# Moving the second attention's first values into the attention, and its row loads to another queue

## The chip, the cores and the metric

The kernel runs on one core of a Trainium2 chip. A core has a matrix engine (TensorE, PE in the profile), three engines for elementwise work (VectorE or DVE, ScalarE or ACT, GpSimd or POOL), and SyncE (SP), which here only issues DMA transfers. Each engine works off its own queue of instructions in order and waits on semaphores for the others. The metric is the device time of one execution in microseconds; the median of several executions is compared.

## The reference

Four blocks run one after the other over x, a matrix of 2048 tokens by 512 features in float32, and each adds its result to x:

```python
x = A_x
x = x + _A_ref(_layernorm(x), A_wqkv, A_wo)
x = x + _B_ref(_layernorm(x), B_wqkv, B_w_phi, B_wo)
x = x + _A_ref(_layernorm(x), A_wqkv, A_wo)
x = x + _B_ref(_layernorm(x), B_wqkv, B_w_phi, B_wo)
```

Block A is softmax attention with 32 heads of 16 features:

```python
qkv = (x @ wqkv).reshape(B, S, 3, H, Dh)           # -> q, k, v by head
scores = einsum("bhqd,bhkd->bhqk", q, k) * Dh ** -0.5
o = einsum("bhqk,bhkd->bhqd", softmax(scores), v)
return o.reshape(B, S, D) @ wo
```

Block B is linear attention. Each head's q and k are mapped by a 16 x 16 matrix w_phi and then by two softmaxes over the 16 features, of the value and of its negative; the state phi_k^T V is 32 x 16 for each head, and the output is phi_q times the state over phi_q times the sum of phi_k, again followed by a product with wo.

## The kernel before

The program has five stages: a preparation with the first layer norm, the first attention (`a1.attention`), the first feature layer (`b1.flow`), the second attention (`a2.attention`) and the last feature layer (`b2.flow`). A generic path behind a condition at the end isn't run on these inputs. Values are kept as a high and a low half in fp16, and a product is three passes (high·high, low·high, high·low), so a product of a 128 x 512 block by four chunks of 128 features is 12 matmuls.

**Attention.** Heads are worked in four octets of eight heads, each as two pairs of half octets ("kq" tiles, group number g from 0 to 7). A step (g, j) takes 512 queries and goes over 16 tiles of 128 keys. For each key tile and each half, `scores` (L1425) writes 128 keys x 2 heads x 512 queries into a pair of PSUM banks, ScalarE takes the exponential into an SBUF tile (L1431, the ring `p` of nine tiles), and `pvs` (L1471) multiplies it with the values. A few of the exponentials are instead computed on VectorE by a polynomial (`power_task`). The kq tiles have 49 rows for each head: 48 rows of high and low halves of the projected keys and queries, which DMAs gather from a staging tile `stg` (`load_rows`, L1402, three DMAs for each of four row groups), and one row with a shift, a bound on the largest score (`load_shift`, L1410). For octet 0 the keys and queries from column AHEAD = 1536 on live in separate small tiles (`kqe`).

The order of all engines inside an attention is written by a planner in the kernel's own Python: it holds estimated costs (`UNIT`, `STEP`, `EXP` and so on), looks 2.6 us ahead and chooses between the next score, the next product with the values, half of one, or a unit of side work. Side work comes from generators (`self.more(...)`): projections of the next octets, the output product of finished tokens, preparation of weights. The strings `LEADS`, `MORES`, `IDLES` and `VBUSY` hold one character for each of the 32 steps (g, j) and each attention: how far ahead a VectorE exponential is placed, the price of an idle TensorE, and how busy VectorE may be.

**Feature layer.** `flow` is a second planner. Each piece of work is a generator that yields an engine ("T" TensorE, "V" VectorE, "A" ScalarE, "P" GpSimd, "D" SP's queue) and a cost; the planner takes the due piece with the lowest rank. The ranks (`RANKS`, `TAIL`, `LAGS`) and strings that put single halves on VectorE or GpSimd (`LOWS`, `ADDS`, `SHARES`, `HALVES`) or choose TensorE, VectorE or GpSimd for a transpose (`TURNS`) are tables. SP isn't one of the engines that this planner orders by itself: its instructions are ordered by the framework below.

The first feature layer ends with the handoff to the second attention. For each block j of 512 tokens: the output product (L2421), the sum into `xt`, layer norm statistics, the normalized rows `xn` (L657 on ScalarE), their transpose into `xnTb` (by TensorE, L670, with ScalarE's high part L680 and VectorE's low part L683; or as an fp16 pair `xh` by a DMA transpose from SP, L2510), the projection of keys and queries of octet 0 (`projected`, L1048, 12 matmuls each), ScalarE's copy `tq` (L2544), VectorE's high and low halves into `stg` (L2547, L2550), ScalarE's squares (L1247). `bounds` sums the squares (L1279), takes the largest (L1285), computes the shift (L1269) and loads it; `rows` loads the kq tiles of the first pair in pieces. `octet_values` projects the values of octet 0 (`values0`, L1233: 48 matmuls of 128 x 128 columns for each j) and copies them out on ScalarE (L1240).

The change touches the planners' tables at the top, `values0`, `values0_out`, the start and the inner choices of `attention`, and `out_block`, `octet_values`, `bounds` and `rows` in `flow`.

## Time and profile before

| what | us |
|---|---|
| median of 3 runs | 2376.18 (2371.74 to 2377.59) |
| the profiled execution, its own time | 2368.89 |
| its span, first to last instruction | 2367.0 |
| TensorE, VectorE, ScalarE, GpSimd busy | 2233.4, 1838.1, 2109.9, 412.0 |

Busy times are sums of records; a matmul's record also covers the time in which it overlaps its neighbours, so a TensorE that is 94% busy isn't 94% used. A row of the order in time gives the start in us from the beginning of the span, the duration, the engine, the source line, the operation, what it writes and reads, and how many equal instructions are merged; in square brackets stand the idle time before it and the work that ended it. A row of groups gives the busy time in us and the mean of one in ns. The profile's chain of waits is empty for this execution, so chains are followed here by hand, from row to row. Line numbers are those of the kernel before; the changed file has its lines three or more further down.

### The profile page before, as it was taken

The page shows a single profiled execution, that of the slowest core. Times are in us where ns is not written, and L with a number is a line of the kernel's source. Part 1 is how long each engine was busy: PE and PEld are TensorE (multiplying, and loading weights), DVE is VectorE, ACT ScalarE, POOL GpSimd, SP SyncE. Part 2 cuts the span into 40 slices and gives each one's busy share as a digit, 9 for nine tenths or more (in the row PEclk, how much of TensorE's full clock was granted, in tenths as well). Part 3 has the DMA queues.
Part 4 walks back from the last instruction along what each step waited for, and adds up shares of the span by engine and source line. Part 5 has one row for each costly group of instructions (what it writes and reads, how often), then busy time and mean ns, then how long its engine had stood idle before and what let it go on. Part 6 is the DMA issues. An engine that isn't in the chain of part 4 may idle for free.

```text
span 2367.0 us, 116770 instructions
## 1 busy us (share of the span) xinstructions
PE 2233.4 (94%) x53046; PEld 1183.4 (50%) x53046; DVE 1838.1 (78%) x2905; ACT 2109.9 (89%) x2415; POOL 412.0 (17%) x536
## 2 busy tenths in 40 slices
PE   6999999999999999999789999999999999999988
PEld 4555555544545554455445554555455545454443
DVE  8567646989687778899855798789977777568997
ACT  6899999999999999766658999999999999996663
POOL 3100000000000000289750000000000000004975
PEclk9999999999999999999999999999999999999999
DMA  5410431123133632143353003302310531223334
GB/s 192 83 23 8 83 53 53 31 45 69 52 66 76 197 94 83 47 107 81 87 129 56 16 17 48 45 4 45 46 45 13 107 115 55 74 67 95 68 59 136
DMA packets 241922, 163.92 MB, mean 69 GB/s; under 512 B 151832, under 2 KB 219016, under 8 KB 240520
## 3 DMA queue, kind: packets, MB, share of 16 engines
q1 hardware_dynamic: 240232, 153.60, 28.8%
q8 instruction: 417, 6.83, 1.2%
q0 software_dynamic: 1184, 2.77, 0.3%
q14 instruction: 89, 0.73, 0.1%
HBM read 62.16 MB, written 41.94 MB: 44 GB/s over the span
## 4 chain that ended last, share of the span: by engine, by line


## 5 line engine op out<-in xcount | busy, mean ns | idle before, releaser
L1425 PE MATMUL s<-kq 49*32 49x512 f16 x14688 | 774.8, 381 | 63.3 <-ACT p__1018 L1431 3.9
L1425 PEld LDWEIGHTS <-kq 49*32 49x32 f16 x15872 | 381.2, 89 | 686.1 <-issue 570.1
L1178 POOL PARTITION_ALL_REDUCE nma<-nmx x6 | 6.3, 1058 | 990.6 <-DVE nmx L1175 815.5
L2062 PEld LDWEIGHTS <-xnTa 128*128 128x128 f16 x1152 | 110.8, 98 | 132.3 <-issue 3.4
L2062 PE MATMUL fl<-wbqk,xnTa 128*128 128x512 f16 x576 | 130.8, 379 | 1.6 <-DVE f L2141 1.6
L1431 ACT ACTIVATE p__1017<-s 128x1024 f32<-128x1024 f32 x119 | 127.8, 1074 | 0.3 <-PE s L1425 0.2
L1431 ACT ACTIVATE p__27883<-s 128x1024 f32<-128x1024 f32 x114 | 122.4, 1074 | 1.9 <-PE s L1425 1.6
L1431 ACT ACTIVATE p__1020<-s 128x1024 f32<-128x1024 f32 x114 | 122.5, 1075 | 0.0
L1431 ACT ACTIVATE p__27887<-s 128x1024 f32<-128x1024 f32 x112 | 120.9, 1079 | 1.7 <-PE s L1425 1.6
L1431 ACT ACTIVATE p__27884<-s 128x1024 f32<-128x1024 f32 x112 | 120.4, 1075 | 1.1 <-PE s L1425 1.0
L1431 ACT ACTIVATE p__27882<-s 128x1024 f32<-128x1024 f32 x112 | 120.5, 1075 | 1.1 <-PE s L1425 1.0
L1431 ACT ACTIVATE p__27881<-s 128x1024 f32<-128x1024 f32 x109 | 117.3, 1076 | 3.7 <-PE s L1425 3.6
L1431 ACT ACTIVATE p__1016<-s 128x1024 f32<-128x1024 f32 x110 | 118.1, 1073 | 1.3 <-PE s L1425 1.0
L1431 ACT ACTIVATE p__1019<-s 128x1024 f32<-128x1024 f32 x110 | 118.1, 1074 | 0.8 <-PE s L1425 0.6
L1431 ACT ACTIVATE p__1018<-s 128x1024 f32<-128x1024 f32 x108 | 116.4, 1078 | 2.0 <-PE s L1425 1.9
L1431 ACT ACTIVATE p__1021<-s 128x1024 f32<-128x1024 f32 x109 | 116.8, 1071 | 0.2
L1431 ACT ACTIVATE p__1022<-s 128x1024 f32<-128x1024 f32 x108 | 115.8, 1073 | 0.4 <-PE s L1425 0.3
L1431 ACT ACTIVATE p__27885<-s 128x1024 f32<-128x1024 f32 x104 | 111.3, 1070 | 2.6 <-PE s L1425 2.5
L1431 ACT ACTIVATE p__27886<-s 128x1024 f32<-128x1024 f32 x104 | 111.7, 1074 | 0.7 <-PE s L1425 0.4
L1431 ACT ACTIVATE p__1015<-s 128x1024 f32<-128x1024 f32 x103 | 110.6, 1074 | 1.8 <-PE s L1425 1.6
L1431 ACT ACTIVATE p__27889<-s 128x1024 f32<-128x1024 f32 x101 | 108.7, 1076 | 0.0
L1509 DVE SCALAR_TENSOR_TENSOR xt<-double,c_oA,xt 128x512 f32<-128x512 f32 x72 | 53.5, 743 | 70.5 <-PE double L771 69.5
(701 smaller groups left out, 7213.0 us busy)
## 6 DMA issues: line engine op xcount, KB each, us to landing
kq<-stg SPq DMA_DIRECT2D x168, 128.0 KB
xd<-xt SPq DMA_DIRECT2D x112, 128.0 KB
xt<-xd SPq DMA_DIRECT2D x80, 128.0 KB
xt<-xd SPq DMA_DIRECT2D x20, 512.0 KB
v<-vyt SPq DMA_DIRECT2D x384, 16.0 KB
oD<-osp SPq DMA_DIRECT2D x48, 128.0 KB
ob<-oD SPq DMA_DIRECT2D x48, 128.0 KB
xd<-xt SPq DMA_DIRECT2D x12, 512.0 KB
```

The costliest lines, as they stand in the source:

```text
L1178: nc.gpsimd.partition_all_reduce(mm, m, P, bass_isa.ReduceOp.max)
L1425: nc.tensor.matmul(banks2[u][32 * c:32 * c + 32, :], self.side(g, half, 64 * u, 0, kt * P + 32 * c, 32), self.side(g, half, 64 * u, 1, j * ...
L1431: nc.scalar.activation(pt, s, AF.Exp, scale=EXPS)
L1509: nc.vector.scalar_tensor_tensor(xt[:, u, :], ps[h], con["oA"], xt[:, u, :], op0=ALU.mult, op1=ALU.add)
L2062: nc.tensor.matmul(ps, xnT[:, a, c, t * P:(t + 1) * P], w(b, c), start=(i == 0 and c == 0), stop=(i == 2 and c == NC4 - 1))
```

## The change

1. The values of octet 0 of the second attention are no longer projected in the first feature layer. `octet_values` is gone, and `attention` of the second layer starts its side work with a new generator `first_values`: four pieces of 12 matmuls for each j, and a copy on VectorE instead of ScalarE. The planner lets a product with the values wait for the block that it needs.
2. The row loads and the shift's constant half for the first pair (`rows`) go out on ScalarE's queue, the third piece on ScalarE's and GpSimd's; they were on SP's and, for that piece, SP's and GpSimd's. `rows` gets the lowest rank (2000 instead of 0).
3. SP's queue takes part in the feature planner: DMA issues yield "D" with a cost, for row loads, shift loads, xt loads and stores.
4. The attention's strings have two characters for each step instead of one (64 instead of 32), and all tables have new values. In the first attention 978 exponentials stay on ScalarE; in the second it is 966 instead of 967.

```diff
-TURN, FOLD = 0.85, 1.15
+TURN, FOLD, VALUE = 0.85, 1.15, 0.85
...
-LOWS = "VVVVPPPPPPVPVVVP", "VVVVVVVPVVVPVPPV"
+LOWS = "VVVVPPPPPPVPVVVP", "PVPVVVPPVVPPPVPV"
...
-HALVES = "VPPPPPPPPPPPVPPP", "PPPPPPPPPPPPPPPP"
-TURNS = "VTPPPTTTPTVTPPVVTTTT", "TPPTVPPTVTVPPPVPPPTP"
+HALVES = "VVPPPPPPPPPPVPPP", "PPPPPVPPPPPPPPPP"
+TURNS = "TTPVTTTTVVVTVTTTTTTT", "VPPPTTTTTVPPPPTTVVPP"
...
+        def first_values(self):
+
+            for j in range(NJ):
+                yield "M", 4
+                idx, ps = self.take()
+                for t in range(4):
+                    yield "pe", VALUE, True
+                    self.values0(j, ps[0], (t,))
+                self.spawn(self.first_out(j, idx, ps))
+
+        def first_out(self, j, idx, ps):
+
+            yield "V", 0.61, 0
+            self.values0_out(j, ps[0], nc.vector.tensor_copy)
+            self.freed(idx)
+            self.done[("v", j)] = self.plan.end + 0.15
...
+            if self.li:
+                self.more(self.first_values())
             for o in (1, 2, 3):
                 self.more(self.octet(o))
...
-                        vnext = [[(G, kt, 0), (G, kt, 1)] for G, kt in islice(pvq, 4)]
+                        vnext = [[(G, kt, 0), (G, kt, 1)] + [("v", kt // 4)] * (self.li and G < 2 * NJ) for G, kt in islice(pvq, 4)]
...
-            def octet_values(j):
-                yield known(state_, "begun")
-                yield known(halves, (j, 0), (j, 1))
-                b = yield "T", 2.75, "one"
-                nxt.values0(j, one(b))
-                yield "A", 0.5
-                nxt.values0_out(j, one(b))
-                F.give_bank(b)
...
-                        nxt.load_shift(0, slice(0, AHEAD), None, (1,), (nc.sync, nc.gpsimd))
+                        yield from shift_of(0, slice(0, AHEAD), None, (1,), "SG")
+                        state_["first"] = F.end + 2.0
...
-                nxt.load_rows(0, slice(AHEAD, S), nxt.kq_end)
-                nxt.load_shift(0, slice(AHEAD, S), nxt.kq_end)
+                yield from rows_of(0, slice(AHEAD, S), nxt.kq_end)
+                yield from shift_of(0, slice(AHEAD, S), nxt.kq_end)
...
+            ISSUE = dict(S=nc.sync, G=nc.gpsimd, A=nc.scalar)
+
+            def rows_of(g, sl, tiles=None, queues="S"):
+                stg = nxt.oct[g // 2]["stg"]
+                for t, r, h8 in nxt.pair_rows(g, tiles, sl):
+                    src = stg[h8 * DH:(h8 + 1) * DH, :, sl]
+                    q = queues[(r // 64) % len(queues)]
+                    if q == "S":
+                        yield "D", 1.95
+                    elif q == "A":
+                        yield "A", 0.6
+                    for n, part in enumerate((slice(1, 3), slice(1, 4, 2), slice(0, 3, 2))):
+                        ISSUE[q].dma_start(t[r + 16 * n:r + 16 * n + 16], src[:, part, :])
...
             def rows():
                 yield known(evac, *[(j, ten) for j in (0, 1) for ten in (1, 0)])
+                yield "D", 2.5
                 nxt.next_w = nxt.octet_w(1)
                 yield F.got(2, "big")
                 F.take("big"), F.take("big")
-                nxt.load_head(False)
+                nxt.alloc_pairs(0)
+                nxt.oct[0]["sh"] = nxt.shift_tile()
+                yield from rows_of(0, slice(0, 1024), None, "A")
+                yield from shift_of(0, slice(0, AHEAD), None, (0,), "A")
                 yield known(evac, (2, 1), (2, 0))
-                nxt.load_rows(0, slice(1024, AHEAD), None, (nc.sync, nc.gpsimd))
+                yield from rows_of(0, slice(1024, AHEAD), None, "AG")
...
-                    F.add(rows(), 0)
+                    F.add(rows(), 2000.0)
...
-                        F.add(octet_values(j), rank("values", j))
```

`shift_of` does for the shift row what `rows_of` does for the rows, at "D" 0.72 or "A" 0.2 for each DMA.

Three places show how instructions move. The first is ScalarE's queue at the handoff, before the change, from the copies of the last block's rows on (xh: fp16 rows for a DMA transpose, tq: projected keys or queries, sq: squares, v: first values):

```order
L2504 ACTIVATE xh<-xn 128x512
L2544 ACTIVATE tq_27618<-fm_24209,c_qk 128x512
L680 ACTIVATE xnTb_2_27579<-fm_24209 128x4x128
L1247 ACTIVATE sq<-stg 128x512
L2544 ACTIVATE tq_27657<-fl,c_qk 128x512
L1247 ACTIVATE sq<-stg 128x512
L2544 ACTIVATE tq_27675<-fm_24209,c_qk 128x512
L1247 ACTIVATE sq<-stg 128x512
L2544 ACTIVATE tq_27729<-fl,c_qk 128x512
L1247 ACTIVATE sq<-stg 128x512
L1240 ACTIVATE v_25865<-fm_24209 128x16x32 x2
L1431 ACTIVATE p__27881<-s 128x1024
```

and now, from the last pair of normalized rows on (L2637 and L2648 are the row and shift loads, L2574 is tq, L2534 is xh, L684 the high part of a TensorE transpose):

```order
L661 ACTIVATE xn<-xt,lb,ly 128x512 x2
L2637 DMA kq_0_27510<-stg 16x2x1024 x3
L2534 ACTIVATE xh<-xn 128x512
L2574 ACTIVATE tq_27548<-fm_24231,c_qk 128x512
L2637 DMA kq_0_27510<-stg 16x2x1024 x3
L684 ACTIVATE xnTb_2_27482<-fm_24230 128x4x128
L1268 ACTIVATE sq<-stg 128x512 x2
L2637 DMA kq_1_27511<-stg 16x2x1024 x6
L2648 DMA kq_0_27510<-sh 1x3x512 x2
L2648 DMA kq_1_27511<-sh 1x3x512 x2
L2574 ACTIVATE tq_27603<-fm_24230,c_qk 128x512
L1268 ACTIVATE sq<-stg 128x512
```

Sixteen DMA issues stand between the last normalized rows and the first of the last two products; another product, its squares and six more row loads follow, and then the first exponential. The copies of the values are gone.

The second place is SP's queue there. Before, from the first pair's row loads on (kq_0_27558 and kq_1_27559 are the first pair, kq_0_27851 the second):

```order
L1402 DMA kq_0_27558<-stg 16x2x1024 x6
L1402 DMA kq_1_27559<-stg 16x2x1024 x6
L1410 DMA kq_0_27558<-sh 1x3x512 x2
L1410 DMA kq_1_27559<-sh 1x3x512 x2
L2510 DMA_TRANSPOSE xnTb_2_27579<-xh 128x8x128 x2
L1402 DMA kqe<-stg 16x2x512 x12
L1410 DMA kqe<-sh 1x16x32 x2
L1402 DMA kq_0_27558<-stg 16x2x512 x3
L1402 DMA kq_1_27559<-stg 16x2x512 x3
L1410 DMA kqe<-sh 1x16x32 x2
L1410 DMA kq_0_27558<-sh 1x3x512
L1410 DMA kq_1_27559<-sh 1x3x512
```

and now (first pair kq_0_27510 and kq_1_27511, second pair kq_0_27681):

```order
L2648 DMA kqe<-sh 1x16x32 x2
L2540 DMA_TRANSPOSE xnTb_2_27482<-xh 128x8x128 x3
L2637 DMA kqe<-stg 16x2x512 x12
L2648 DMA kqe<-sh 1x16x32 x2
L1431 DMA kq_0_27681<-sh 1x4x512 x2
L205 DMA wA<-dA 128x512 x4
L1423 DMA kq_0_27681<-stg 16x4096
L1423 DMA kq_0_27681<-stg 16x2x2048
L2648 DMA kq_0_27510<-sh 1x3x512
L2648 DMA kq_1_27511<-sh 1x3x512
```

The transposes of the last block stand ahead of all row loads; the first pair's last shift rows stand behind the kqe rows, four weight loads and two loads of the second pair.

The third place is VectorE at the start of the second attention, before (sh: the shift; vyt: values of octet 1):

```order
L1294 TENSOR_REDUCE top<-nmt 1x1
L1266 TENSOR_SCALAR okt<-top 1x1
L1268 TENSOR_SCALAR neg<-top 1x1
L1269 TENSOR_SCALAR sh<-sh,neg 1x512
L1120 COPY vyt_28060<-double 128x512
L1122 TENSOR_TENSOR vyt_28060<-vyt_28060,double 128x512
```

and now:

```order
L1290 TENSOR_SCALAR sh<-sh,neg 1x512
L1261 COPY v_25858<-double 128x16x32
L1261 COPY v_25858<-pm_27832 128x16x32
L1261 COPY v_25858<-pm_27942 128x16x32
L1261 COPY v_25858<-pm_28021 128x16x32
L1124 COPY vyt_28443<-pm_28111 128x512
L1126 TENSOR_TENSOR vyt_28443<-vyt_28443,pm_28112 128x512
```

Four copies of the first values stand ahead of octet 1's. On TensorE, whose rows alternate with weight loads, the first values stand behind the first score: nine scores with eight groups of 12 matmuls between them, a product with the values, two scores, 48 matmuls, a product, two scores, 48 matmuls, a product.

61 lines of the change are left out of this document (41 added, 20 removed).

## The prediction

> **What bounds the kernel now.** I read the table of stages first, then the waits of ScalarE, then the order in time of every queue across the handoff from the first feature layer to the second attention. The five stages are cut at the first and last exponential of each attention. The columns are the window, its length, the busy time of TensorE, its weight loads, VectorE, ScalarE and GpSimd, the granted TensorE clock, the DMA share and the rate.
>
> ```profile
> 71.50:980.70 909.20, 875.25 (x24374) 468.83 (x24374) 663.15 (x1049) 901.56 (x978) 12.57 (x29) 1.00 0.29 66
> 980.70:1246.20 265.50, 240.47 (x2185) 123.80 (x2191) 228.81 (x383) 157.28 (x242) 198.70 (x279) 0.97 0.41 92
> 1246.20:2148.80 902.60, 867.47 (x24311) 458.50 (x24299) 690.89 (x1018) 891.98 (x967) 12.86 (x25) 1.00 0.24 51
> 2148.80:2367.00 218.20, 200.67 (x1832) 98.25 (x1820) 196.84 (x307) 118.88 (x169) 162.37 (x143) 0.96 0.39 89
> ```
>
> Both attentions are bound by ScalarE: 978 and 967 exponentials fill 901.56 of 909.20 and 891.98 of 902.60 us, 0.922 us each in the second, which leaves 10.6 us of idle time there. The two feature layers are bound by no single engine. The first is 265.5 us long, and its end is a chain of waits:
>
> ```profile
> 1223.30:1229.50 6.20, 0.00 (x0) 0.00 (x0) 1.12 (x2) 1.30 (x2) 0.00 (x0) 0.75 0.48 92
> 1229.50:1246.20 16.70, 14.33 (x148) 8.98 (x156) 5.72 (x18) 3.83 (x6) 4.82 (x14) 0.89 0.30 54
> ```
>
> For 6.2 us TensorE does nothing, and afterwards it runs at a lower clock. What it waits for stands in SP's queue (start, duration, what was issued):
>
> ```profile
> 1214.02 7.83 SPq L1402 DMA_DIRECT2D kq<-stg  x12
> 1221.95 2.89 SPq L1410 DMA_DIRECT2D kq<-sh  x4
> 1224.95 2.66 SPq L2510 DMA_TRANSPOSE xnTb<-xh  x2
> 1227.72 7.82 SPq L1402 DMA_DIRECT2D kqe<-stg  x12
> ...
> 1243.30 1.40 SPq L1410 DMA_DIRECT2D kq<-sh  x2
> 1244.74 0.56 SPq L1402 DMA_DIRECT2D kq<-stg  x1
> ```
>
> Twelve row loads take 0.65 us each to issue, and the same 0.65 us for half the bytes (kqe), so it is the issue that costs, not the transfer. A shift load takes 0.72, a transpose 1.33. The last two transposes of the last block's normalized rows stand behind 16 loads that nothing needs yet. On TensorE:
>
> ```profile
> 1220.00 0.66 PE L670 MATMUL fm<-ident,xn 128*128 128x128 f32 x4
> 1220.49 2.75 PE L1048 MATMUL fl<-xnTb,wA 128*128 128x512 f16 x12
> 1229.55 4.56 PE L1048 MATMUL fm<-xnTb,wA 128*128 128x512 f16 x12 [6.30 <-DMA xnTb<-xh]
> 1233.95 2.75 PE L1048 MATMUL fl<-xnTb,wA 128*128 128x512 f16 x12
> 1236.54 2.84 PE L1233 MATMUL fm<-wAv,xnTb 128*128 128x128 f16 x48
> 1239.31 0.82 PE L1279 MATMUL fl<-sq,bones 128*32 128x512 bf16 x3
> ...
> 1245.56 0.80 PE L1425 MATMUL s<-kq 49*32 49x512 f16 x16 [2.32 <-DVE sh L1269]
> ```
>
> The keys' projection waits 6.30 us for those transposes and then takes 4.56 us where its twins take 2.75. The values of one block (48 matmuls, 2.77 us from start to start) stand ahead of the norms (L1279) that give the bound, without which no score can start. On ScalarE:
>
> ```profile
> 1217.33 1.52 ACT L657 ACTIVATE xn<-xt,lb,ly 128x512 f32<-128x512 f32 x2 [0.46 <-POOL lb L2464]
> ...
> 1234.15 0.69 ACT L2544 ACTIVATE tq<-fm,c_qk 128x512 f32<-128x512 f32 x1 [9.06 <-PE fm L1048]
> ...
> 1237.92 0.63 ACT L1247 ACTIVATE sq<-stg 128x512 bf16<-128x512 f16 x1 [0.49 <-DVE stg L2547]
> ...
> 1246.20 1.02 ACT L1431 ACTIVATE p__27881<-s 128x1024 f32<-128x1024 f32 x1 [2.65 <-PE s L1425]
> ...
> 1260.71 1.02 ACT L1431 ACTIVATE p__27885<-s 128x1024 f32<-128x1024 f32 x1
> ```
>
> I call the end of the last pair of normalized rows Z, here 1217.33 + 1.52 = 1218.85. From Z to the first exponential are 27.35 us, and this is the stretch that the change rewrites.
>
> **The change, part by part.** *The handoff after Z.* Three chains now race, and the latest decides.
>
> The work itself: a TensorE transpose, ScalarE's high part and VectorE's low part take from 1220.00 to the end of this row, 2.47 us:
>
> ```profile
> 1221.80 0.67 DVE L683 TENSOR_TENSOR xnTb<-fm,xnTb 128x512 f16<-128x512 f32 x1
> ```
>
> Then 12 matmuls, 2.75. So the first of the last two products is ready at Z+5.3 (before: 1234.15, Z+15.3). From there to the first exponential it took 12.05 us, of which the norms lost 0.76 behind the values (last square done 1237.92 + 0.63 = 1238.55, norms 1239.31); without them 11.3. That is Z+16.6, a gain of 10.7 us.
>
> ScalarE's queue: between the last xn and that product it has sixteen issues, six row loads ahead of the high part, then six more and four shift loads. The trace has no DMA issue on ScalarE. The lower bound is nothing on the path (it issues while it would wait), the upper is SP's price for each, 12 × 0.65 + 4 × 0.72 = 10.7, or more if the queues disturb each other. GpSimd's own row loads are nearest beside SP's:
>
> ```profile
> 1238.18 3.22 POOL L1402 DMA_DIRECT2D kq<-stg  x6 [18.39 <-DVE stg L2547]
> ```
>
> that is 0.54 each. I take SP's price, since it is the same kind of queue, and a start when the xn pair starts (Z-1.5): the product is then read at Z+9.2, and the first exponential comes at Z+20.5.
>
> SP's queue: from about Z+1.5 (the last fp16 half) it issues one transpose, twelve kqe rows, four shift loads (kqe and the next pair), six larger loads (four weights, two rows of the next pair), and only then the shift row that the first score needs: 1.33 + 12 × 0.65 + 4 × 0.72 + 6 × 0.56 + 0.72 = 16.1, so Z+17.6. Before, the score came 0.86 after these issues (1243.30 + 1.40 to 1245.56), and the exponential 0.64 after the score: Z+19.1, and up to 1.5 more, since that shift load waits for a load ahead of it to land.
>
> Both queues say Z+19 to Z+21; I take Z+20.2, a gain of 7.1, with ends of 10.7 (queues free) and -6 (queues disturb each other, below).
>
> *Ahead of Z.* TensorE loses one projection and one block of values before the last output product, 2.75 + 2.77, and gets three transposes more, 3 × 0.66: 3.5 us less. VectorE gets one more low half of the queries and two more low parts of transposes, by these rows:
>
> ```profile
> L2263 DVE TENSOR_TENSOR fq<-f,fq 128x1024 f16<-128x1024 f32 x2 | 2.9, 1450 | 0.0
> ...
> L683 DVE TENSOR_TENSOR xnTb<-fm,xnTb 128x512 f16<-128x512 f32 x4 | 2.6, 678 | 0.0
> ```
>
> 1.45 + 2 × 0.68 = 2.8 us more, while two divisions move to GpSimd. VectorE has 228.81 of 265.5 us to do and no cover over long stretches, so Z moves by -3.5 to +2.8; I take -1.
>
> *First values inside the second attention.* Four blocks of 48 matmuls, 11.1 us by the 2.77, move behind the first score. In the new order nine scores alternate with eight quarters of a block; then come a product with the values, two scores, a whole block, and the same again. The rates (a product of all 512 columns is two halves):
>
> ```profile
> 1250.75 0.54 PE L1425 MATMUL s<-kq 49*32 49x512 f16 x8
> 1250.97 0.74 PE L1471 MATMUL pm<-p__27881,v 64*32 64x512 f32 x4
> ...
> 1251.83 0.54 PE L1425 MATMUL s<-kq 49*32 49x512 f16 x8
> ```
>
> Score 0.22, product 0.86, quarter 0.69, block 2.77. The 14th score starts 9 × 0.22 + 8 × 0.69 + 3 × 0.86 + 4 × 0.22 + 2 × 2.77 = 16.5 us after the first, and its exponential 0.64 later: 17.1, against 1260.71 - 1245.56 = 15.15 now. So +2.0. The rest of the 11.1 us takes the place of the next octet's values, which start later and are due far later. The cover is TensorE's slack; if it is gone, ScalarE pays all 11.1. The four copies out of the bank go from ScalarE to VectorE, which is busy 690.89 of 902.6 us. One exponential fewer stands on ScalarE (966): -0.9.
>
> *Tables.* The first attention keeps 978 exponentials and the same order over its first 600 scores: 0, at most 1 either way. In the last layer VectorE gives four low halves of values to GpSimd (4 × 0.68 by the row of their shape) and takes one of queries (1.45): 1.3 less on an engine busy 196.84 of 218.2 us, where GpSimd fills up. I take -0.5, bounds -2.5 and +1.5.
>
> The sum is -1 - 7.1 + 2.0 - 0.9 - 0.5 = -7.5. I round it to -7, for the rest of the tables can only lose what nobody has seen. The profiled execution took 2368.89 (span 2367.0) and would take 2362; the median of the three runs is 7.3 above it, so the forecast for the median is 2376.18 - 7 = 2369.2.
>
> **Rivals.** *The queues are no hindrance:* ScalarE's sequencer issues in its waits, SP overtakes. Then 10.7 after Z and 3.5 ahead of it: -3.5 - 10.7 + 2.0 - 0.9 - 0.5 = -13.6, 2362.6. For it speaks that ScalarE works 157.28 of 265.5 us there; against it, that SP's order is fixed and long.
>
> *The issues on ScalarE and SP hold each other up.* From Z-1.5 on sixteen issues on ScalarE and some twenty on SP stand side by side, and each queue's loads wait on loads of the other. If they go out one at a time, 36 × 0.65 = 23.4 us, ScalarE reads the first product at about Z+22 and the first exponential comes at Z+33: 6 later than now, in all -1 + 6 + 2.0 - 0.9 - 0.5 = +5.6, 2381.8. It decides from about 1.1 us per issue on ScalarE on: sixteen of them then end at Z+16, and the gain is gone. For it speaks SP's timeline, where twelve issues stand end to end from 1214.02 to 1221.85 and nothing overlaps; against it, that the six loads on GpSimd at 1238.18, issued while SP was issuing too, took no longer each than SP's. [...]
>
> *TensorE has no slack in the attention:* it is busy 867.47 of 902.6 us, so ScalarE waits for all 11.1 us: -1 - 7.1 + 11.1 - 0.9 - 0.5 = +1.6, 2377.8. Against it: those records overlap (the score row lasts 0.54, but the next starts after 0.22), and ScalarE idles only 10.6 us now.
>
> *The handoff is gated elsewhere anyway:* the order of the SP queue isn't what the code asks for, and the bound's shift row lands late, say at Z+25. Gain 2.3 there: -2.4 in all, 2373.8.
>
> **How the numbers follow.** What a measurement of this kernel can tell from no change is about 0.3%, 7.1 us. The forecast gets 0.45 (from -11 to -3, half of it beyond -7.1), the free queues 0.20, the gated handoff 0.15, no slack 0.08, queues in each other's way 0.12 (-1 to +12, half of it beyond +7). Faster: 0.20 + 0.23 = 0.43; slower: 0.06, and 0.04 for tables that go wrong in stages that I took at 0: 0.10; the same: 0.47. The range reaches from the free queues to just short of the queues in each other's way, 2361 to 2380; the forecast's own is 2365 to 2373.
>
> **What would show it.** Right: no wait of TensorE for a transpose at the handoff, first exponential 19 to 21 us after Z, ScalarE's issues at 0.6 to 0.7 us, the first values as 192 short matmuls behind the first score, about 5 us of ScalarE's idle time among its first 14 exponentials, and 966 of them in 904 us. Wrong: issues on ScalarE near 0.2 us with the first exponential before Z+18, or above 1.1 us with one after Z+27; a second attention longer than 908 us; a Z that moved by more than 4 us; a last layer that moved by more than 3.

## The result, and where the time went

The changed kernel takes 2394.23 us (median of four, 2391.45 to 2399.25), the kernel before 2376.89 beside it. The ratio is 1.0091 (95% interval 1.0079 to 1.0104): slower by 17 us by the medians and 22 by the ratio, where I had forecast 7 us less. The stages of the changed kernel, cut as before at the first and last exponential of each attention:

```profile
71.74:994.12 922.38, 879.79 (x24405) 471.20 (x24406) 663.67 (x1052) 902.28 (x978) 12.69 (x29) 0.99 0.29 65
994.12:1268.52 274.40, 234.05 (x1995) 114.57 (x1994) 234.88 (x388) 155.87 (x237) 192.13 (x274) 0.93 0.38 88
1268.52:2182.67 914.15, 876.39 (x24760) 472.49 (x24762) 700.00 (x1023) 891.18 (x966) 12.18 (x25) 0.99 0.24 50
2182.67:2397.50 214.83, 199.53 (x1828) 97.81 (x1816) 194.01 (x305) 121.54 (x172) 164.78 (x145) 0.96 0.41 92
```

Against before: the first attention +13.3 us (922.4 for 909.1, with the same 978 exponentials), the first feature layer +8.9 (Z comes 243.9 us after the end of the attention, not 238.2; from Z to the first exponential 30.5, not 27.4), the second attention +11.5 with one exponential fewer, the last layer -3.4. With 0.2 ahead of the first exponential that sums to 30.5 us: this profiled execution is the longest of its kernel (2399.25) and the one of before was a short one (2368.89), so some 10 us of it are chance. Part of this lies in the first attention: the kernel before and seven of the kernels below have the same instructions there, in the same order on ScalarE, VectorE, GpSimd and SP, and take 909.1 to 915.2 us.

*The two attentions.* The waits of ScalarE and VectorE name two places. First ScalarE's, then VectorE's rows, then SP's queue at the first place, in the changed kernel (the line numbers are 4 to 21 higher than before's, 30 in the feature layer):

```profile
818.81 1.02 ACT L1452 ACTIVATE p__1020<-s 128x1024 f32<-128x1024 f32 x1 [7.23 <-PE s L1446]
1949.66 1.03 ACT L1452 ACTIVATE p__27717<-s 128x1024 f32<-128x1024 f32 x1 [7.33 <-PE s L1446]
```

```profile
815.44 1.29 DVE L1462 TENSOR_SCALAR px<-pm 128x512 int32<-128x512 f32 x2 [10.40 <-DMA wbqk<-dBqk]
...
1946.29 1.29 DVE L1462 TENSOR_SCALAR px<-pm 128x512 int32<-128x512 f32 x2 [9.37 <-DMA xd<-xt]
```

```profile
802.74 8.03 SPq L205 DMA_DIRECT2D wbqk<-dBqk  x14
810.86 2.17 SPq L205 DMA_DIRECT2D xd<-xt  x2
```

VectorE starts an exponential of its own in a buffer (px) that comes out of the same ring as the tiles of x (xt). The rows of an earlier xt are still to be stored, and the store stands behind fourteen weight loads that take 8.03 us to issue. VectorE waits 10.40 us, TensorE finds its bank not emptied, and ScalarE loses 7.23 us. The second attention has a wait of the same kind at 1946.29; the store is issued at 1943.44 there, 6.5 us after the rows were summed, behind weight loads and other loads and stores. The longest wait at such a row in the attentions of before is 1.81 us.

*The handoff.* ScalarE's queue and its work, then SP's queue, then TensorE, all of the changed kernel:

```profile
1236.54 0.72 ACTq L2637 DMA_DIRECT2D kq<-stg  x1
1237.26 0.80 ACT L661 ACTIVATE xn<-xt,lb,ly 128x512 f32<-128x512 f32 x1
...
1242.86 1.36 ACTq L2637 DMA_DIRECT2D kq<-stg  x2
...
1246.11 1.31 ACTq L2637 DMA_DIRECT2D kq<-stg  x2
1249.42 0.59 ACTq L2637 DMA_DIRECT2D kq<-stg  x1
1250.44 0.59 ACTq L2637 DMA_DIRECT2D kq<-stg  x1
1252.10 1.25 ACTq L2637 DMA_DIRECT2D kq<-stg  x2
1253.44 3.70 ACTq L2648 DMA_DIRECT2D kq<-sh  x4
1257.24 0.69 ACT L2574 ACTIVATE tq<-fm,c_qk 128x512 f32<-128x512 f32 x1 [11.35 <-DMA wA<-dA]
...
1268.52 1.02 ACT L1452 ACTIVATE p__27711<-s 128x1024 f32<-128x1024 f32 x1 [7.77 <-PE s L1446]
...
1289.78 1.03 ACT L1452 ACTIVATE p__27715<-s 128x1024 f32<-128x1024 f32 x1 [2.30 <-PE s L1446]
```

```profile
1239.17 4.50 SPq L2540 DMA_TRANSPOSE xnTb<-xh  x3
1243.77 7.83 SPq L2637 DMA_DIRECT2D kqe<-stg  x12
```

```profile
1246.33 4.72 PE L1052 MATMUL fm<-xnTb,wA 128*128 128x512 f16 x12 [7.57 <-DMA xnTb<-xh]
...
1267.56 0.86 PE L1446 MATMUL s<-kq 49*32 49x512 f16 x8 [4.38 <-DVE top L1315]
1268.35 1.46 PE L1254 MATMUL double<-wAv,xnTb 128*128 128x128 f16 x12
...
1274.21 0.84 PE L1254 MATMUL double<-wAv,xnTb 128*128 128x128 f16 x12
```

The transposes are all issued by Z+5.6 (before: Z+8.8; Z is 1238.06 here), but TensorE still waits 7.57 us for them, and the first product is ready at 1251.05, Z+13.0, where I had said Z+5.3. It is read only at 1257.24, Z+19.2, since ScalarE's sixteen issues last from 1236.54 to 1257.14. The issues themselves are not slow: each of the twelve row loads takes 0.59 to 0.73 us on ScalarE, and SP's twelve beside them keep their 0.65. The time goes by between them: 3.45 us before 1242.86, 1.89 before 1246.11, then 2.00, 0.43 and 1.07 among the last six. In the trace the loads of SP and ScalarE signal on the same eight semaphores (GpSimd's on eight others), and these issues carry a wait on the semaphore that they then use. By the landings in the trace, the issues at 1249.42, 1250.44 and 1252.10 go out 0.02 us after the kqe load of SP that used their semaphore last has landed, that at 1242.86 as long after one of SP's transposes, and that at 1246.11 as long after ScalarE's own load of 1242.86. From the read product to the first exponential it is 11.28 us; I had said 11.3. The 14th exponential starts 21.26 us after the first, where before had 14.51: a quarter of a block takes 1.46 us at first and 0.84 later, and the granted clock of the changed kernel says why:

```profile
1253.60:1257.10 3.50, 0.04 (x1) 0.06 (x1) 0.00 (x0) 0.00 (x0) 0.00 (x0) 1.00 0.49 124
1257.10:1274.20 17.10, 8.82 (x72) 4.56 (x71) 5.64 (x18) 5.59 (x7) 4.82 (x14) 0.50 0.43 76
...
1276.50:1279.00 2.50, 2.50 (x50) 1.68 (x48) 0.00 (x0) 2.50 (x3) 0.00 (x0) 1.00 1.17 125
```

The clock falls to 0.50 at 1257.1, 3.5 us into TensorE's wait for tq, stays there through the norms and the wait of 4.38 us behind them, and is 0.50 for the first 6.6 us of the scores. In before, too, it is 0.59 over the first 3.8 us of the second attention.

### The profile page after: what moved, and what is told of

The parts are those of the page before. It is cut to its first block, busy times and chain, and to the rows that moved or that the text cites. A ratio compares the mean times of both kernels' runs of the same rounds, so it can differ in the third digit from the quotient of the medians.

```text
span 2397.5 us, 117355 instructions
## 1 busy us (share of the span) xinstructions
PE 2238.4 (93%) x53346; PEld 1188.8 (50%) x53346; DVE 1850.8 (77%) x2915; ACT 2111.0 (88%) x2412; POOL 407.2 (17%) x533
## 4 chain that ended last, share of the span: by engine, by line
ACT 40%; PE 30%; DVE 12%; issue 10%; POOL 5%; SPq 2%; DMA 1%; ACTq 0%; DVEq 0%; POOLq 0%
PE s L1446 7%; PE double L1492 6%; PE pm L1492 5%; ACT p__1016 L1452 3%; ACT p__1020 L1452 2%; ACT p__1017 L1452 2%; PE pm L775 2%; ACT p__1019 L1452 2%; ACT p__1018 L1452 2%; ACT p__27716 L1452 2%; ACT p__1023 L1452 2%; ACT p__1021 L1452 2%; ACT p__1022 L1452 2%; ACT p__27717 L1452 2%; ACT p__27713 L1452 2%
## 5 line engine op out<-in xcount | busy, mean ns | idle before, releaser
L1452 ACT ACTIVATE p__1020<-s 128x1024 f32<-128x1024 f32 x115 | 123.5, 1074 | 8.0 <-PE s L1446 8.0
L1452 ACT ACTIVATE p__27711<-s 128x1024 f32<-128x1024 f32 x113 | 121.2, 1073 | 8.9 <-PE s L1446 8.8
L1452 ACT ACTIVATE p__1017<-s 128x1024 f32<-128x1024 f32 x118 | 126.6, 1073 | 2.1 <-PE s L1446 1.9
L1452 ACT ACTIVATE p__27716<-s 128x1024 f32<-128x1024 f32 x118 | 126.6, 1073 | 1.1 <-PE s L1446 1.1
L1452 ACT ACTIVATE p__1016<-s 128x1024 f32<-128x1024 f32 x116 | 124.5, 1073 | 2.0 <-PE s L1446 1.7
L1452 ACT ACTIVATE p__27713<-s 128x1024 f32<-128x1024 f32 x114 | 122.3, 1073 | 3.5 <-PE s L1446 3.4
L1452 ACT ACTIVATE p__27717<-s 128x1024 f32<-128x1024 f32 x110 | 118.2, 1074 | 7.8 <-PE s L1446 7.7
L1452 ACT ACTIVATE p__1021<-s 128x1024 f32<-128x1024 f32 x111 | 119.0, 1072 | 1.4 <-PE s L1446 1.2
L1452 ACT ACTIVATE p__27719<-s 128x1024 f32<-128x1024 f32 x110 | 118.2, 1075 | 0.7 <-PE s L1446 0.5
L1452 ACT ACTIVATE p__27718<-s 128x1024 f32<-128x1024 f32 x108 | 115.9, 1074 | 0.8 <-PE s L1446 0.7
L1452 ACT ACTIVATE p__1018<-s 128x1024 f32<-128x1024 f32 x106 | 113.9, 1075 | 2.5 <-PE s L1446 2.5
L1452 ACT ACTIVATE p__27715<-s 128x1024 f32<-128x1024 f32 x104 | 111.6, 1073 | 4.4 <-PE s L1446 4.2
L1452 ACT ACTIVATE p__1022<-s 128x1024 f32<-128x1024 f32 x106 | 113.6, 1072 | 2.0 <-PE s L1446 1.9
L1452 ACT ACTIVATE p__1019<-s 128x1024 f32<-128x1024 f32 x106 | 113.6, 1072 | 0.8 <-PE s L1446 0.6
L1452 ACT ACTIVATE p__1015<-s 128x1024 f32<-128x1024 f32 x103 | 111.0, 1077 | 1.8 <-PE s L1446 1.7
L1452 ACT ACTIVATE p__27714<-s 128x1024 f32<-128x1024 f32 x98 | 104.9, 1071 | 2.5 <-PE s L1446 2.2
L1452 ACT ACTIVATE p__1023<-s 128x1024 f32<-128x1024 f32 x97 | 104.0, 1072 | 0.5 <-PE s L1446 0.3
L2087 PE MATMUL fl<-wbqk,xnTa 128*128 128x512 f16 x444 | 101.2, 379 | 0.0
```

What stands on the lines that cost most here:

```text
L1452: nc.scalar.activation(pt, s, AF.Exp, scale=EXPS)
L2087: nc.tensor.matmul(ps, xnT[:, a, c, t * P:(t + 1) * P], w(b, c), start=(i == 0 and c == 0), stop=(i == 2 and c == NC4 - 1))
```

## The experiments

Times are medians; each ratio is to the kernel before, run beside it. The stages are those of one profiled execution each: "Z" is counted from the end of the first attention, "to exp" from Z to the first exponential.

| kernel | us | ratio (95%) | att. 1 | Z | to exp | att. 2 (exps) | last |
|---|---|---|---|---|---|---|---|
| before | 2376.89 | | 909.1 | 238.2 | 27.4 | 902.6 (967) | 218.2 |
| changed | 2394.23 | 1.0091 (1.0079-1.0104) | 922.4 | 243.9 | 30.5 | 914.2 (966) | 214.8 |
| q_sp | 2394.65 | 1.0093 (1.0077-1.0108) | 919.0 | 242.8 | 27.4 | 915.5 (966) | 214.7 |
| q_pool | 2404.76 | 1.0122 (1.0105-1.0138) | 923.9 | 243.5 | 36.3 | 915.9 (966) | 214.9 |
| w_pool | 2385.02 | 1.0047 (1.0033-1.0060) | 914.2 | 243.5 | 30.5 | 909.3 (966) | 215.0 |
| act_rows | 2377.23 | 1.0021 (1.0012-1.0030) | 910.6 | 251.0 | 23.6 | 899.5 (967) | 217.9 |
| fv_only | 2387.92 | 1.0065 (1.0052-1.0079) | 910.5 | 242.7 | 31.2 | 913.2 (974) | 216.9 |
| old_exp | 2387.71 | 1.0065 (1.0051-1.0078) | 910.7 | 242.5 | 31.2 | 910.7 (974) | 215.1 |
| old_flow | 2400.15 | 1.0123 (1.0107-1.0139) | 918.8 | 245.2 | 23.5 | 911.9 (966) | 224.4 |
| late | 2366.13 | 0.9976 (0.9966-0.9987) | 910.4 | 238.3 | 22.9 | 899.8 (967) | 216.9 |
| warm | 2382.28 | 1.0041 (1.0028-1.0055) | 913.4 | 237.7 | 27.5 | 910.5 (974) | 217.2 |
| no_fv | 2403.73 | 1.0131 (1.0115-1.0146) | 918.9 | 253.3 | 20.8 | 917.0 (976) | 219.7 |
| late_f2 | 2366.67 | 0.9980 (0.9971-0.9989) | 911.8 | 238.5 | 21.2 | 903.1 (967) | 217.1 |
| late_f2w | 2367.29 | 0.9976 (0.9964-0.9987) | 911.4 | 238.9 | 21.1 | 904.9 (967) | 216.8 |
| mended | 2396.15 | 1.0108 (1.0094-1.0123) | 911.1 | 251.8 | 19.1 | 922.2 (966) | 217.0 |
| mended_cold | 2393.70 | 1.0095 (1.0080-1.0110) | 911.7 | 242.4 | 24.3 | 918.7 (966) | 217.7 |
| fv_warm | 2396.98 | 1.0107 (1.0092-1.0121) | 915.2 | 244.4 | 34.6 | 911.1 (974) | 216.5 |
| fv_fill | 2390.35 | 1.0078 (1.0065-1.0091) | 911.8 | 239.5 | 35.4 | 910.9 (974) | 218.2 |
| mended2 | 2382.61 | 1.0038 (1.0024-1.0052) | 912.7 | 243.3 | 25.0 | 914.1 (966) | 217.2 |

**The loads of the handoff on another queue, in the changed kernel: q_sp, q_pool.**

```diff
-            ISSUE = dict(S=nc.sync, G=nc.gpsimd, A=nc.scalar)
+            ISSUE = dict(S=nc.sync, G=nc.gpsimd, A=nc.sync)      # q_sp;  A=nc.gpsimd: q_pool
```

> The changed kernel, with the sixteen loads that it issues from ScalarE's queue at the handoff (and the six behind them) put on SP's queue; the order on TensorE, VectorE and ScalarE is the same. In the changed kernel ScalarE is held from 1236.54 to 1257.14 us by these issues (1.21 us each beside SP's, 0.6 to 0.8 alone) and reads the first of the last two products 19.2 us after the last normalized rows (Z). Theory: an issue on ScalarE costs its own time and more beside SP's, and blocks the evacuations. Then this kernel's ScalarE is free, but SP has 16 issues more ahead of the last transposes (10.7 us at 0.65 each), so the end of the handoff moves from Z+30.5 to about Z+27, as in the kernel before: 3 us less than the changed kernel. Rival: what counts is the number of issues, on whatever queue, since they go out one at a time: no difference, Z+30. The two long stalls of VectorE in the attentions stay in both cases.

> The changed kernel, with the same loads on GpSimd's queue. GpSimd issued six such loads in 3.21 us (0.54 each) while SP was issuing too. Theory (ScalarE's queue and SP's hold each other up, GpSimd's does not): ScalarE reads the first product at about Z+8 and the first exponential comes 19 to 21 us after Z, where the changed kernel has 30.5: some 10 us less in all. Rival (issues go out one at a time whatever the queue): SP's twelve loads get slower than 0.65 each and the first exponential stays at Z+28 or later: within 3 us of the changed kernel.

On SP the profile does what the theory says: tq is read 15.3 us after Z and the first exponential comes at Z+27.4. The time is that of the changed kernel all the same (1.0093 for 1.0091), as the rival has it; 3 us are near what these runs can tell apart, so this run decides nothing. On GpSimd both were wrong: it is 7 us slower by the ratios, 10 by the medians. GpSimd issues its loads in 0.54 each, but SP's transposes beside them take 1.33, 3.12 and 4.70 us to issue, where the changed kernel has 1.28 to 1.71, and the keys' projection waits 13.57 us (SP, GpSimd, TensorE of q_pool):

```profile
1240.11 9.30 SPq L2540 DMA_TRANSPOSE xnTb<-xh  x3
```

```profile
1238.78 5.95 POOL L2637 DMA_DIRECT2D kq<-stg  x11
```

```profile
1253.27 5.28 PE L1052 MATMUL fm<-xnTb,wA 128*128 128x512 f16 x12 [13.57 <-DMA xnTb<-xh]
```

**The loads alone on ScalarE, in the kernel before: act_rows.**

```diff
-            self.load_rows(0, slice(0, 1024))
+            self.load_rows(0, slice(0, 1024), None, (nc.sync,) if every else (nc.scalar,))
...
-                nxt.load_rows(0, slice(1024, AHEAD), None, (nc.sync, nc.gpsimd))
+                nxt.load_rows(0, slice(1024, AHEAD), None, (nc.scalar, nc.gpsimd))
```

(and the shift loads behind the first likewise)

> The kernel before, with only its row loads (and the four shift loads behind them) moved from SP's queue to ScalarE's at the same place of its program; compute order as before. Theory: SP's last transposes come up to 10 us earlier, but ScalarE's issues beside SP's cost 0.7 to 1.2 us each and block it for 15 to 20 us, so the first exponential comes 27 to 32 us after Z (before: 27.35): 0 to 5 us slower than the kernel before. Rival (the queue change is a gain by itself, and the loss of the changed kernel comes from its tables alone): first exponential 17 to 22 us after Z, 5 to 10 us faster than before.

5 us slower, as the theory had it, but by another way: the issues block ScalarE ahead of Z, so Z comes 12.8 us later, and the rest is shorter. ScalarE's queue of act_rows, with the normalization that stands behind the issues:

```profile
1215.44 5.38 ACTq L1402 DMA_DIRECT2D kq<-stg  x8
1223.23 2.52 ACTq L1402 DMA_DIRECT2D kq<-stg  x4
1229.30 0.81 ACT L657 ACTIVATE xn<-xt,lb,ly 128x512 f32<-128x512 f32 x1 [13.11 <-DMA kq<-sh]
```

Each issue takes 0.59 to 0.72 us, so the price that I had taken from SP holds on ScalarE. Between the eighth and the ninth it waits 2.41 us; a shift load of SP, issued at 1220.70, landed at 1223.20, 0.03 us ahead of the ninth. Put ahead of Z, even issues at that price hold the normalization up by 13.11 us.

**Weight loads off SP's queue: w_pool; the old exponentials' tables: old_exp** (both from the changed kernel; old_exp has MORES, IDLES and VBUSY of before in the same way, each sign doubled).

```diff
-            spread(self.wqk.rearrange(...), dBqk.rearrange(...), 8, 2)
+            spread(self.wqk.rearrange(...), dBqk.rearrange(...), 8, 2, nc.gpsimd)     # w_pool
...
-LEADS = ("bb775577777777777799777766aa7777aa557777a97777446777550077000000", ...)
+LEADS = ("bb775577777777777799777766aa7777aa557777aa7777447777550077000000", ...)    # old_exp
```

> The changed kernel, with the sixteen loads of the second layer's query and key weights (wbqk) issued from GpSimd's queue instead of SP's, in both attentions; the planned order is the same but for these. Theory: VectorE's waits of 10.40 us at 815.44 and 9.37 us at 1946.29 are waits for a buffer whose rows are still to be stored, and the store stands in SP's queue behind those loads (1 load each 0.6 us); each costs ScalarE 7.2 to 7.3 us. Without the loads ahead of it the store goes out some 8 us earlier, both stalls nearly vanish, and the kernel gets 12 to 15 us faster than the changed one, some 2380. Rival: the stores land late for another reason (the transfers themselves, or the loads ahead of these): the stalls stay, and less than 4 us is won.

> The changed kernel with the exponentials' tables of before (each entry written twice), all else as changed; it has 974 exponentials in the second attention instead of 966. Theory: the stall at 815 us in the first attention comes from the new tables, which start a task of VectorE where its buffer's rows still wait in SP's queue behind sixteen weight loads: with the old tables the first attention takes 909 to 912 us again instead of 919 to 924, and the second loses its stall of 7 us but gets 7 us of exponentials. In all some 10 us faster than the changed kernel. Rival (the stall comes with the first half of the program for another reason, the tables are innocent): the first attention stays above 917 us.

Both show the cause in the first attention, and both win less than expected: w_pool 10 us by the ratios instead of 12 to 15, old_exp 6 instead of 10. In w_pool the store is issued at 801.72 with no weight load ahead, VectorE's wait is gone in the first attention and still 6.06 us in the second, where loads of ob remain in the queue, and ScalarE waits 0.66 and 3.41 us in place of 7.23 and 7.33:

```profile
801.72 2.87 SPq L205 DMA_DIRECT2D xd<-xt  x4
```

```profile
1933.02 1.29 DVE L1462 TENSOR_SCALAR px<-pm 128x512 int32<-128x512 f32 x2 [6.06 <-DMA ob<-oD]
```

With the old tables the first attention is at 910.7. Between the 780th and the 840th exponential the changed kernel loses 8.0 us to before; q_sp, q_pool, no_fv and old_flow, the other four with the new tables and those loads on SP, lose 7.0 to 9.1, and the thirteen without the one or the other at most 0.9.

**The move of the first values alone, in the kernel before: fv_only.**

```diff
+            if self.li:
+                self.more(self.first_values())
...
-                        F.add(octet_values(j), rank("values", j))
```

(with the new functions first_values, first_out and values0 of the change)

> The kernel before, with only the first values moved into the second attention (queues and tables of before; the planner then gives ScalarE 974 exponentials there instead of 967). Theory: their cost is paid at the start of the attention, where TensorE runs at a low clock after the wait of the handoff: the 14th exponential starts 5 to 7 us later after the first than the 14.51 us of before, of which 4 to 5 us stay; the seven exponentials add 6.4 us; the handoff gets 2 to 4 us shorter without the values. In all 5 to 10 us slower than before. Rival (TensorE has the slack, the move is free or a gain): the 14th exponential at most 3 us later, the attention at most 909 us, the kernel within 3 us of before or faster.

The loss is larger than the theory's, 15.5 us: 6.4 for seven exponentials, 4.2 for the rest of the attention as expected, but the feature layer is 8.4 us longer, not shorter, though it has 192 matmuls fewer. My first reading was TensorE's clock (0.63 and 0.83 in stretches of 20 us where before had 0.83 and 1.00).

**Is it the clock? warm, fv_warm, fv_fill.** All three are fv_only with matmuls added into a bank that nobody reads.

```diff
+                b = yield "T", 2.75, "one"          # warm: planned, at the old places
+                nxt.values0(j, one(b))
...
+                if not ten:                         # fv_warm: unplanned, all else in fv_only's order
+                    nxt.values0(j, one(b))
                 run(nxt.project(0, j, one(b), ten, 12))
...
+                for j in (0, 1):                    # fv_fill: behind the last norms
+                    nxt.values0(j, one(b))
```

> The kernel before with the first values moved into the second attention, as in the run of that move alone, but the old 192 matmuls are still done in the feature layer at their old places too, into a bank that nobody reads. So it does strictly more work than that run. Theory: TensorE's granted clock falls where it is left without work (0.63, 0.83 and 0.67 in stretches where before had 0.83, 1.00 and 0.84), and that, not the order, is why Z came 4.5 us later and the handoff took 31.2 us. With the matmuls back the clock is at 0.8 to 1.00 there, Z is back at 237 to 240 us after the end of the first attention, Z to the first exponential takes 26 to 29 us, and the kernel is 4 to 8 us faster than with the move alone in spite of the added work. Rival (the order of the move delays the path, the clock does not matter): Z at 242 to 246, no gain.

> The kernel before with the move of the first values alone (Z 242.7 us after the first attention, 31.2 from Z to the first exponential), and the old 192 matmuls put back unplanned, 48 ahead of each block's projection of the queries, into the bank that this projection then overwrites. The order of everything else on TensorE, VectorE, ScalarE and GpSimd is the same as with the move alone, so only the load on TensorE (11 us more) and its clock change; in the earlier run with these matmuls the planned order had changed too. Theory (the clock costs it): Z 237 to 241, as with the values in place, granted clock 1.00 in the stretches that had 0.83 and 0.93. Rival (the order costs it, the clock does not): Z at 242 or more, later by what the matmuls take.

> The same move alone, with 96 matmuls into a bank nobody reads behind the last norms, where TensorE otherwise waits 5.51 us for the shift row ahead of the first score. Theory: with them the clock is 1.00 at the first scores, a score and a quarter of a block take 1.11 us instead of 1.95, and the 14th exponential starts 18.5 to 19 us after the first instead of 20.68; the first exponential comes at most 1 us later. Rival (the low clock there has another cause, or the matmuls delay the first score): still above 20 us, or the first exponential 2 us later or more.

warm looks like a proof: Z at 237.7, 27.5 to the first exponential, 5.6 us faster with more work. fv_warm takes most of the proof back: with the order of fv_only held on all engines but SP and the same matmuls, Z is at 244.4 and the handoff at 34.6, and the kernel is 9 us slower than fv_only (in the profiled executions the feature layer is 5.1 us longer, and the first attention, which is the same in both, 4.7). Most of what warm had restored was the plan. What moved is SP's queue. Its rows of before, fv_only and warm, from the last transposes ahead of the row loads on:

```profile
1212.51 1.41 SPq L2510 DMA_TRANSPOSE xnTb<-xh  x1
1214.02 1.39 SPq L1402 DMA_DIRECT2D kq<-stg  x2
```

```profile
1220.59 4.57 SPq L2529 DMA_TRANSPOSE xnTb<-xh  x3
1225.27 0.72 SPq L1419 DMA_DIRECT2D kq<-stg  x1
```

```profile
1216.98 1.63 SPq L2529 DMA_TRANSPOSE xnTb<-xh  x1
1218.71 7.81 SPq L1419 DMA_DIRECT2D kq<-stg  x12
```

In fv_only one more of the late transposes stands ahead of the row loads, which start 241.9 us after the first attention instead of 233.4 (warm 233.1). And from the first row load to the first exponential it is 32.2 us in before, 32.0 in fv_only, 32.0 in warm, 32.5 in fv_warm: in these four the feature layer ends as long after the start of SP's chain (12 loads, 4 shifts, transposes, 12 loads more, 6, a shift), with or without the added matmuls. In fv_fill, whose matmuls stand right ahead of the first score, it is 36.0.

fv_fill shows what the clock does cost, at two places. The 14th exponential starts 18.74 us after the first instead of 20.68, so 2 us; but the matmuls wait for VectorE and take 7.00 us, and the first score, at 1258.66, waits for them, which costs more:

```profile
1251.61 7.00 PE L1250 MATMUL fl<-wAv,xnTb 128*128 128x128 f16 x96 [3.29 <-DVE nm L1302]
```

Up to the last norms it is fv_only instruction for instruction, and yet its Z is 3.2 us earlier. The rows name the reason. TensorE waits the same 3.78 us for VectorE in both, and the same 24 matmuls of the output product follow; a row and the window of the 24, first of fv_only, then of fv_fill:

```profile
1197.85 1.44 PE L2440 MATMUL fm<-wbo,obB 128*128 128x512 f16 x3 [3.78 <-DVE xt L2452]
1197.80:1206.20 8.40, 8.15 (x24) 3.00 (x24) 2.16 (x5) 0.75 (x3) 4.70 (x16) 0.66 0.58 154
```

```profile
1198.58 0.81 PE L2440 MATMUL fm<-wbo,obB 128*128 128x512 f16 x3 [3.78 <-DVE xt L2452]
1198.50:1204.10 5.60, 5.34 (x24) 2.34 (x24) 2.17 (x6) 0.73 (x3) 4.61 (x16) 1.00 0.88 224
```

They take 8.40 us at a granted clock of 0.66 and 5.60 at 1.00. So the first reading was right in part: of the 8.5 us by which the row loads start later in fv_only than in before, 3 are the clock of that execution (in fv_fill they start at 238.9) and 5.5 the order. fv_warm waits 3.49 us at this place and has 0.76 behind it, so it did not hold the clock up where it counted.

**The row loads behind the transposes, still on SP, in the kernel before: late.**

```diff
             def rows():
                 yield known(evac, *[(j, ten) for j in (0, 1) for ten in (1, 0)])
+                yield known(state_, *[("t", j, t) for j in range(NJ) for t in range(4)])
```

(the transposes leave their planned time in state_; nothing else is changed)

> The kernel before, with the row loads still on SP's queue but planned after the last transposes (ten of twelve then stand behind them, and the loads of the last columns, kqe, behind all that the first score needs); nothing else changed. Theory: what the handoff needs is the transposes ahead of the loads, not another queue: TensorE's wait of 6.30 us shrinks to 1 to 3 us, the first exponential comes 21 to 23 us after Z instead of 27.35, and the kernel gets 4 to 6 us faster than before. Rival (the loads themselves are what the first score waits for, and they now end later): first exponential at 26 us or more after Z, no gain.

6.3 us faster than before by the medians, 5.7 by the ratio, as the theory said; none of the kernels here is faster. SP's queue, then TensorE:

```profile
1221.33 1.26 SPq L2510 DMA_TRANSPOSE xnTb<-xh  x1
1222.68 1.38 SPq L1402 DMA_DIRECT2D kq<-stg  x2
1224.15 1.32 SPq L2510 DMA_TRANSPOSE xnTb<-xh  x1
1225.52 6.33 SPq L1402 DMA_DIRECT2D kq<-stg  x10
1231.95 2.91 SPq L1410 DMA_DIRECT2D kq<-sh  x4
1235.77 4.00 SPq L1402 DMA_DIRECT2D kq<-stg  x6
1240.65 1.49 SPq L1410 DMA_DIRECT2D kq<-sh  x2
1242.19 3.85 SPq L1402 DMA_DIRECT2D kqe<-stg  x5
```

```profile
1227.53 4.44 PE L1048 MATMUL fm<-xnTb,wA 128*128 128x512 f16 x12 [2.33 <-DMA xnTb<-xh]
...
1242.89 0.87 PE L1425 MATMUL s<-kq 49*32 49x512 f16 x16 [1.79 <-DMA kq<-sh]
```

TensorE's wait of 6.30 us is 2.33, the chain from the first row load is 20.8 us instead of 32.2, and the kqe loads that the first score does not need come last. In the profiled executions 4.3 us are won up to the first exponential and 2.8 in the second attention, whose first 14 exponentials take 11.89 us instead of 14.51: the granted clock is 1.00 there, where before has 0.59. act_rows, with 1.00 there too, takes 11.86.

**The other parts: old_flow, no_fv, late_f2, late_f2w.**

```diff
-RANKS = dict(heads=(-175.6, -274.9, 74.4, -110.2), out=(83.8, 351.5, -71.4, 137), ...    # old_flow, from the changed kernel
+RANKS = dict(heads=(-86.2, -138.2, 12.5, -32.5), out=(75.3, 254.8, 25.2, 87.4), ...
...
-                self.more(self.first_values())          # no_fv, from the changed kernel
+                        F.add(octet_values(j), rank("values", j))
...
-TURNS = "VTPPPTTTPTVTPPVVTTTT", "TPPTVPPTVTVPPPVPPPTP"          # late_f2, from late
+TURNS = "VTPPPTTTPTVTPPVVTTTT", "VPPPTTTTTVPPPPTTVVPP"
```

(old_flow has all tables of the feature layers of before, late_f2 those of the last layer of the change; late_f2w is late_f2 with the edit of w_pool)

> The changed kernel with the ranks, shares and turns of the feature layers of before. Theory: the 5.5 us by which the last normalized rows came later after the end of the first attention (243.5 instead of 238.2 us) come from these tables: they are back at 236 to 240, and the last layer loses its gain of 3.4 us. Rival (the loads that ScalarE and the planner now hold cost it, as when only the loads were moved and Z came at 251.0): Z stays at 242 us or more after the end of the first attention.

> The changed kernel with the first values back in the first feature layer, as in the kernel before; its new tables, ranks and queues stay (the planner then gives ScalarE 976 exponentials in the second attention instead of 966, 9.2 us more). Theory: the move of the values is the larger part of the loss, so Z comes at 236 to 240 us after the end of the first attention instead of 243.5, and the 14th exponential starts 12 to 15 us after the first instead of 21; with the ten exponentials the kernel is 0 to 6 us faster than the changed one. Rival (the queues and ranks delay Z): Z stays at 242 us or more.

> The kernel before with the row loads planned after the last transposes (that alone gave a ratio of 0.9976), and the shares, turns and ranks of the last feature layer taken from the changed kernel. Theory: the last layer's 3.4 us of gain (214.8 instead of 218.2) are its tables', and independent of the rest: the last layer takes 214 to 216 us, and the ratio to the kernel before is 0.996. Rival (that gain came from the other costs that the planner has in the changed kernel): the last layer at 217 us or more, the ratio stays at 0.9976.

> The same, with the sixteen weight loads of the feature layers' queries and keys issued from GpSimd's queue. Theory: where no store is waited for, taking these loads off SP's queue wins little: 0 to 2 us less than without it. Rival (SP's queue delays more than those stores in the attentions): 4 us or more.

old_flow: Z does not come back (245.2), so the new tables are not what delays it, and the last layer gets 6 us longer than before. no_fv: Z does not come back either; its row loads start at 233.6, early again, but on ScalarE ahead of the normalization, and Z is at 253.3 as in act_rows. Its first exponential comes as late as the changed kernel's (274.1 us after the first attention for 274.4), and ten exponentials more make it slower. late_f2: the last layer takes 217.1, so its gain of 3.4 us does not come with the tables alone; what of the change brings it was not found. late_f2w: no gain, as expected where no store is waited for.

**The sum: mended, mended_cold, mended2.** The changed kernel with the row loads as in late, the first attention's old tables and the weight loads on GpSimd; mended has warm's matmuls too, mended2 is mended_cold with the last three row loads moved ahead of the second pair's.

```diff
-                yield from rows_of(0, slice(0, 1024), None, "A")
+                yield from rows_of(0, slice(0, 1024), None, "S")
...
-                yield from rows_of(0, slice(1024, AHEAD), None, "AG")
+                yield from rows_of(0, slice(1024, AHEAD), None, "SG")                     # mended, mended_cold
+                nxt.load_rows(0, slice(1024, AHEAD), None, (nc.sync, nc.gpsimd))          # mended2
```

> The changed kernel with every named cause taken away at once: the row loads on SP's queue behind the last transposes, the first attention's exponential tables of before, the weight loads (wbqk) on GpSimd's queue, and the 192 matmuls of the first values done in the feature layer as well, into a bank nobody reads, to keep TensorE's clock up; the first values that count stay in the second attention. If the named causes are all there is, the first attention takes 909 to 912 us, Z comes 236 to 240 us after it, the first exponential 21 to 25 us after Z, the second attention takes 904 to 909, the last layer 214 to 216, and the kernel is level with the one before (2366 to 2378 where that has 2372). If another cause is left in the changed order of work (Z at 242 or more, or the second attention above 911 us), it stays above 2380.

> The same without the added matmuls. Theory (the clock, not the order, costs the time of the move): Z 3 to 6 us later than with them, a granted clock of 0.5 to 0.7 around the first scores, and 4 to 8 us more in all, though 192 matmuls fewer. Rival (in the changed order the clock plays no part): as fast as with them or faster.

> The mended changed kernel without the added matmuls, and without the wait of 11.8 us that the mending itself had brought (three row loads of the first pair stood behind the second pair's in SP's queue; here they are issued ahead). If that wait was an accident of the mending, the second attention takes 905 to 908 us instead of 918.7 and the kernel some 2382 where the one before has 2371, so 10 us of loss stay with first values moved, without the new tables' stall in the first attention and without ScalarE's loads. If instead the attention waits somewhere else, it stays above 912.

mended is 2.4 us slower than mended_cold, within their intervals, and its Z is at 251.8 instead of 236 to 240, so the added matmuls bring nothing here; as the planned order differs between the two, they say no more of the clock. Both had a wait of 11.5 to 12.0 us that the mending brought in (three row loads behind the second pair's in SP's queue). Without it mended2 is 12.6 us faster than the changed kernel by the ratios (1.0091 to 1.0038, of 2372), and still 9 us slower than before: the first attention and the feature layer are mostly repaired (912.7 us, and 268.3 to the first exponential where before has 265.5), but the second attention stays at 914.1, where 905 to 908 was expected, so that the kernel's time fits the 2382 of the expectation by chance. It loses 6 us at its start, 3 at a shorter stall of the same kind (ScalarE waits 3.05 us at 1932.64, VectorE before it 5.32 us for loads of ob), and 3 more in small waits that I did not follow.

## Why the prediction was wrong, step by step

- "*The first attention keeps 978 exponentials and the same order over its first 600 scores: 0, at most 1 either way.*" I compared orders on TensorE and ScalarE and took the rest for harmless; an exponential of VectorE moved to where its buffer hung on a store in SP's full queue: 8.0 of the 13.3 us, shown by w_pool and old_exp, and the other 5.3 are within what kernels with the same first attention differ by (909.1 to 915.2). A wait of the same kind stood in the second attention (7.3), which I had no term for; w_pool took about half of it away. Together they are the largest miss.
- "*I take SP's price, since it is the same kind of queue.*" The price was right (0.59 to 0.73 us for a row load on ScalarE), and so was the start of the issues at Z-1.5. What I put at nothing are the waits between issues, 8.8 us, and 0.9 for a first shift load of 1.58: tq is read at Z+19.2, not Z+9.2. This is what the rival of queues in each other's way named as "each queue's loads wait on loads of the other"; its other premise, that issues go out one at a time, isn't seen: between 1246.11 and 1247.42 two issues of ScalarE and as much as two of SP went out, each in 0.59 to 0.68 us, so issues of the two queues overlapped there. The work itself was misjudged too. Three of the last block's four tiles come by SP's transposes, which are issued by Z+5.6 and land 2.6 us later, and the 12 matmuls take 4.72 us instead of 2.75: the product is ready at Z+13.0, not Z+5.3, and a free ScalarE alone would not have brought the 7.1. So the handoff gained nothing: +3.1 instead of -7.1.
- "*Z moves by -3.5 to +2.8; I take -1.*" It moved by +5.7. This is no chance: seven kernels with the changed order of work up to Z have it at 242.4 to 243.9, four with the order of before at 238.2 to 238.9. Over the last 38 us ahead of Z the clock is 1.00 in the changed kernel, so it isn't lost there; 160 to 180 us after the first attention it is 0.73, where before has 0.91, and may have a share. I had counted engines' work, and less work did not bring the end nearer; which part of the new order costs the 5 us was not found (with the old tables, old_flow, Z stays at 245.2; with SP's row loads behind the transposes, mended2, at 243.3). The end of the whole layer also hangs on SP's chain. I had read this chain (Z+17.6 for its last shift row) and yet counted the values as work on the path.
- "*So +2.0*" for the start of the second attention: the mechanism was right and the size off. In fv_fill, with quarters at 0.84 us from the first on, it is 18.74 us from the first exponential to the 14th, not 16.5 (17.1 from the first score): a score and a quarter take 1.11 us, not 0.91, which I had added from rates of unmixed matmuls. The low clock, which I had seen after TensorE's wait of before and not carried over, adds 2 to 2.5 us; the 14.51 of before has it too, and is 11.9 without it (late, act_rows). ScalarE is 4.6 us late by its 20th exponential, and does not get it back.
- "*-0.5*" for the last layer: -3.4, outside my bounds; open.
- The rival of no TensorE slack is refuted: the loss that comes from the values stays near 4 us of the 11.1. The sum of the gated handoff is -2.7 by its own terms, 2373.5, not -2.4.
- Right: 966 exponentials, and that the transposes no longer wait behind row loads on SP, though TensorE's wait for them grew from 6.30 to 7.57 us. The 11.3 us from the product to the first exponential (11.28) are partly luck: in the changed kernel the second product is ready (1253.64) before the first is read, in before it came 2.5 us after, so the same length is made up of other parts.
